# Linear attention and a routed expert layer in one kernel: the empty rows behind the whole second batch, the ramp's loads by two chunks, the first tokens' load between the two weights' loads, one chain of scales per expert

## The chip, the cores and the metric

The kernel runs on one core of one Trainium2 chip. The metric is the device time of one execution in microseconds; the median of three runs before is 392.27 us (391.34 to 393.69). Times below are in microseconds from the start of the profiled span unless they are durations.

## The reference

For 4 batches, 8 heads, 768 positions and a head size of 48, a gated linear attention runs over the positions, and its output, 3072 tokens of 384 values, goes through a layer of 8 experts, each token through one:

```python
f = 1.0 / (1.0 + np.exp(-f_logit))
for t in range(S):
    state = f[:, :, t, :, None] * state + np.einsum('bhd,bhe->bhde', k[:, :, t], v[:, :, t])
    y[:, :, t] = np.einsum('bhd,bhde->bhe', q[:, :, t], state)
# x = y with the heads side by side: 3072 x 384
e_idx = np.argmax(x @ w_gate, axis=1)          # the token's expert
gate_w = softmax(x @ w_gate)[e_idx]            # its scale, with
eom = sigmoid(x @ w_output_gate)[e_idx]        # the output gate's
h = np.maximum(x[mask] @ w1[e], 0.0)           # 384 -> 1024
out[mask] = gate_w * eom * (h @ w2[e])         # 1024 -> 384
```

## The kernel before

**The attention.** Each batch is cut into 6 chunks of 128 positions, so there are 24 chunks, numbered 0 to 23; chunks 0 to 5 are batch 0. Within a chunk a running product p of the forget gates and its counterpart i are made by scans, k is multiplied by i and q by p, and then the chunk is plain matmuls: scores (`qk`, L245), a causal mask, outputs from the state before and from the scores (`out_y`, L305 and L309), the chunk's contribution to the state (`state`, L278, with k transposed at L262), and a matmul that puts the heads side by side and makes the gates' logits at once (`x_tr`, L322). `prep(t)` holds a chunk's preparations as named steps: `s` (L197, ScalarE's sigmoid of the first position), `f` (L204, ScalarE's sigmoid of the others), `scan_p` and `scan_i` (VectorE), `mul_k` (L220) and `mul_q` (L223), on GpSimd from chunk 3 on.

The loop over t (L462) staggers this: iteration t computes the scores of chunk t, the outputs of chunk t-1 and the copies (`evac_y`, L316), state update (`state_upd`, L290 to L293) and turn of chunk t-2, and prepares t+1 to t+3. All engines keep the order in which the program is written: `chain` (L1047) binds each engine's instructions to it. So an instruction that waits holds back everything behind it on its engine.

**The loads.** All of them are issued on SyncE's queue in the order of the program. `load(b, cuts)` (L169) loads chunks c0 to c1 of the tensors named by letters: f, k, q by heads and positions, v by positions. Batch 0 and 1 are loaded ahead of the loop (L423 to L432), batches 2 and 3 in the loop, from iteration 3 on. Between the parts of batch 1 stand eight stores, one for each expert, that fill slots 256 to 511 of its place in a DRAM buffer `xs_dram` with rows marked empty (`clear`, L646). A DMA on this queue takes one of eight semaphores in turn, so that at most eight are under way.

**The routing.** When a group of chunks is through, each of its tokens has an expert and a slot among the expert's tokens (`route`, `slots`). From iteration 7 on a GpSimd scatter per chunk (`scatter`, L339) writes the chunk's 128 rows into `xs_dram`; it waits for the empty rows. The expert with the most tokens after 16 chunks is taken first; its weights w1 and w2 are loaded (`load(0, ...)`, L399, L609 and L621), four DMAs of 384 KB each, and when the scatters of the first 16 chunks are out, its first 256 tokens (`tokens_in`, L652). Its other tokens are loaded when all scatters have landed.

**The experts.** Weights and tokens are split into a high and a low part (`split`: a ScalarE cast, L631, and a subtraction, L632, on VectorE or GpSimd; `x_split`: L710 and L711), and each product is three matmuls. `mm1` (L754) makes one of 8 hidden blocks, with a ScalarE relu (L758) and a VectorE subtraction (L759) behind it and two PSUM buffers to do it in; `mm2` (L776) takes a hidden block to the outputs. The first expert is done in two parts: its early 256 tokens beside the end of the attention (`x_early`, `mm1_early`), then `AHEAD` blocks of their `mm2`, with the transposes of the late tokens (`x_late`) two blocks before their end, and then the late ones. While an expert's `mm2` runs, a list `front` of steps of the next one (splits of w1, transposes and splits of the tokens by `x_in`, L704) is worked off, one step per block. A token's scale is a chain of 13 small operations over all tokens of an expert (`gain_ops`, L680), mostly VectorE's, worked off a few at a time by `gain`; the first expert has two such chains, one for the early and one for the late tokens.

Of the kernel before, what the change touches and what calls it, by code (L numbers as in the profile page):

```python
# [21 lines left out]
C = 128  # L22
# [4 lines left out]
TS = 128  # L27
NT = 4
SLOTS = NT * TS
# [1 line left out]
EARLY = 256  # L31
T_TOP = 16
T_END = 20
AHEAD = 6
KC = DM // 128
KF = F // 128
BIG = 8192
# [4 lines left out]
RW = LG + 2 * E  # L42
# [3 lines left out]
HELD = 256  # L46
# [81 lines left out]
def attention(ctx, tc, nc, k, kpool, rt, q01, k01, f01, q23, k23, f23, v, wg, xs_dram, r, ex):  # L128
# [204 lines left out]
    def scatter(n):  # L333

        for _ in range(min(n, len(sq))):
            if sq[0] >= T_TOP and not ex.xg:
                return
            t = sq.pop(0)
            i = nc.gpsimd.indirect_dma_start(  # L339
                out=xs_dram, out_offset=bass.IndirectOffsetOnAxis(ap=r.slot[:, t:t + 1], axis=0),  # L340
                in_=xn[t // 4][:, t % 4, :], in_offset=None, bounds_check=E * N - 1, oob_is_err=False)
            for other in ex.apart:
                tc.declare_no_dep(i.ins, other.ins, reason="other slots")
            ex.apart.append(i)

# [42 lines left out]
    def top(ps):  # L388

        key = rt.tile([128, E], F32, name="key")  # L390
        mx = rt.tile([128, 1], F32, name="mx")
        nc.vector.scalar_tensor_tensor(out=key, in0=ps, scalar=float(E), in1=k.first_key, op0=ALU.mult, op1=ALU.add)
        dq[:0] = [
            lambda: nc.vector.tensor_reduce(out=mx, in_=key, axis=AX.X, op=ALU.max),
            lambda: nc.vector.tensor_tensor(out=r.top, in0=key, in1=mx.broadcast_to([128, E]), op=ALU.is_equal),
            lambda: nc.vector.tensor_tensor(out=key, in0=r.top, in1=k.num, op=ALU.mult),
            lambda: nc.vector.tensor_reduce(out=mx, in_=key, axis=AX.X, op=ALU.add),
            lambda: nc.vector.tensor_copy(out=r.top_id, in_=mx),
            lambda: ex.load(0, r.top_id[0:1, 0:1]),  # L399
        ]  # L400

    def slots(gi, t0, n):
# [17 lines left out]
    order = [(b, c) for b in range(B) for c in range(NCH)]  # L420
    last = len(order) - 1
    pre_of = [prep(t) for t in range(len(order))]
    load(0, [("fk", 0, 1), ("f", 1, 2), ("q", 0, 1), ("kq", 1, 2), ("f", 2, 4), ("v", 0, 2)])  # L423
    nc.sync.dma_start(out=turn[:, 0::2, 2 * D:XW], in_=wg[:, 0::2, 0:2 * E])
    for i in range(2):
        nc.sync.dma_start(out=turn[64 * i:64 * i + 64, 1::2, 2 * D:XW],
                          in_=wg[64 - 64 * i:128 - 64 * i, 1::2, 0:2 * E])
    load(0, [("kqv", 2, 4), ("fkqv", 4, 6)])
    load(1, [("fkqv", 0, 2), ("fkqv", 2, 4)])
    for e in range(E):  # L430
        ex.clear(e)
    load(1, [("fkqv", 4, 6)])  # L432

    def pre(t, *names):
        if hot(t):
# [26 lines left out]
    for t in range(last + 1):  # L462
# [3 lines left out]
        fill(more)  # L466
        if hot(t - 2):
            evac_y(t - 2, (1,))
        if t > 0:
            pre(t + 2, "f")  # L470
        if hot(t - 2):
            evac_y(t - 2, (0,))
            state_upd(t - 2)
        pre(t + 1, "mul_k")
        if t + 1 == last:
            done_sb.close()
# [34 lines left out]
            state(t - 1)  # L511
        run_pq(ready)
        if t == last:

            evac_y(t - 1)
            state_upd(t - 1)
            ex.x_early()
            for heads in ((0, 1, 4, 5), (2, 3, 6, 7)):
                out_y(t, heads)
            ex.split(1, 0, 2, nc.gpsimd)  # L520
# [3 lines left out]
        b, c = divmod(t - 3, NCH)  # L524
# [8 lines left out]
        if t >= T_END:  # L533
            scatter(2)
            if len(ex.apart) == T_TOP:
                ex.tokens_in(0, 0, EARLY // TS)
        if t + 1 == last:
            drain()
            assert ex.xg
            ex.split(1, 0, 0, nc.gpsimd)  # L540
# [32 lines left out]
class Experts:  # L573
# [4 lines left out]
    def __init__(self, tc, nc, k, r, raw, right, w1, w2, xs_dram, out, kp):  # L578
        self.tc, self.nc, self.k, self.r, self.raw, self.right, self.kp = tc, nc, k, r, raw, right, kp
        self.w1, self.w2, self.xs, self.out = w1, w2, xs_dram.rearrange("(e n) w -> e n w", e=E), out  # L580
        k.gain = kp.tile([TS, NT, E], F32, name="gain")
        k.dst = kp.tile([TS, NT, E], I32, name="dst")

        self.first = kp.tile([TS, NT, RW], F32, name="first_x")
        self.apart, self.number = [], {}
        self.wr, self.whl, self.todo, self.gq = {}, {}, [], []
        self.xg, self.xt, self.hs, self.ys, self.ysb = {}, {}, {}, {}, {}

# [50 lines left out]
    def clear(self, e):  # L639

        if e == 0:
# [1 line left out]
            self.nc.gpsimd.memset(self.empty, 0.0)  # L643
            self.nc.gpsimd.memset(self.empty[:, DM:DM + 1], float(BIG))
        n = (SLOTS - HELD) // TS
        self.nc.sync.dma_start(out=self.xs[e, HELD:SLOTS].rearrange("(j p) w -> p j w", p=TS),  # L646
                               in_=self.empty.unsqueeze(1).broadcast_to([TS, n, RW]))

    def tokens_in(self, s, j0, j1):
        early = s == 0 and j0 == 0  # L650
# [8 lines left out]
            self.apart.append(i)  # L659
        for j in range(j0, j1):  # L660
            self.xg[s, j] = (t[:, j - j0, :], min(TS, CAPS[s] - j * TS))
        self.meta = getattr(self, "meta", []) + [(s, j0, j1, t)]

    def gains(self):

# [192 lines left out]
    def run(self):  # L858
# [7 lines left out]
        for s in range(E):  # L866
# [7 lines left out]
            for f in range(KF):  # L874
                self.mm1(s, f)
                if s == 0:
                    self.gain(3)
                    if f > 2 and f % 2:
                        self.split(1, 1, f // 2 - 1, self.nc.gpsimd)
                if f % 2 == 0 and (2, s, f // 2) in self.wr:  # L880
                    self.split(2, s, f // 2, self.nc.gpsimd if s == 0 else None)
                if 1 <= f <= len(back):
# [1 line left out]
            front = [lambda i=i: self.split(1, s + 1, i) for i in range(KF // 2)  # L884
                     if (1, s + 1, i) in self.wr]
            for c in range(KC):
                front.insert(2 * c + 2 if s > 0 else len(front), lambda c=c: self.x_in(s + 1, c))
            if s + 1 == E:
                front = []
            self.gain(len(self.gq))  # L890
# [237 lines left out]
```

## Time and profile before

| | before |
|---|---|
| median of three runs | 392.27 us |
| the profiled execution, its span | 394.05 us, 392.3 us |
| granted TensorE clock, mean | 0.982 |
| TensorE busy | 365.1 us (93%) |
| VectorE, ScalarE, GpSimd busy | 235.6, 197.1, 150.7 us |
| moved by DMAs | 67.75 MB |

The profile is of one execution and has a time of its own, so parts of the span are set against 394.05 and not against the median. The attention takes the first 125 us or so, the first expert's early part runs from there to 148, its late part to 176, and the seven other experts the rest. Of the page's slices, the DMA row is at 0.9 from the second to the tenth of 40, and the granted clock at 0.9 or more but for the last.

### The profile page before, as it was taken

The numbers are of one execution on the slowest core, as the hardware profiler recorded it, in microseconds if no ns is written. First come the engines' busy times: TensorE is split into PE (matmuls) and PEld (weight loads), VectorE is DVE, ScalarE is ACT, GpSimd is POOL, SyncE is SP. The second block draws the span as 40 slices with busy tenths as digits, with TensorE's granted clock in tenths as the row PEclk, the third lists the DMA queues.
The fourth block names the chain that finished last, engine by engine and source line by source line (L and its number), as shares of the span: only waits on it lengthen the run. The fifth ranks groups of instructions, "written<-read, shape, count | busy, mean of one in ns | idle before, by whom it ended". The sixth has DMA issues, their size and how long they took to land.

```text
span 392.3 us, 8488 instructions
## 1 busy us (share of the span) xinstructions
PE 365.1 (93%) x3199; PEld 336.6 (86%) x3199; DVE 235.6 (60%) x495; ACT 197.1 (50%) x471; POOL 150.7 (38%) x180
## 2 busy tenths in 40 slices
PE   7799889999996999799999999999999999999990
PEld 3588778898886888799989999999999999999990
DVE  7878669898992764725644645454564565565500
ACT  3576466766754643415534634634644644654310
POOL 7676678899987650501201210310210310321011
PEclk9999989999999999989999999999999999999996
DMA  8999999999167139632535453544454454520010
GB/s 232 349 360 355 285 258 217 294 251 289 70 205 265 45 126 313 215 124 72 161 119 162 144 167 125 178 133 160 144 161 144 141 160 145 161 79 34 2 43 19
DMA packets 53427, 67.75 MB, mean 173 GB/s; under 512 B 3954, under 2 KB 48005, under 8 KB 53376
## 3 DMA queue, kind: packets, MB, share of 16 engines
q1 hardware_dynamic: 50064, 57.46, 50.0%
q0 software_dynamic: 3312, 9.65, 6.9%
q8 instruction: 27, 0.44, 0.5%
q14 instruction: 24, 0.20, 0.2%
HBM read 54.16 MB, written 13.39 MB: 172 GB/s over the span
## 4 chain that ended last, share of the span: by engine, by line
PE 65%; DMA 11%; DVE 6%; issue 6%; SPq 5%; POOL 3%; ACT 2%; POOLq 0%; DVEq 0%; ACTq 0%
PE h_ps L754 25%; PE y_ps L776 21%; PE y_ps L790 4%; SPq L182 4%; DMA f_t<-in_f 3%; PE x_ps L704 3%; PE x_ps L322 2%; DMA xs_dram<-empty 2%; PE o_ps L811 2%; DMA out<-o,dst 2%; DMA v_t<-in_v 2%; PE a_ps L245 2%; POOL xs_dram L339 2%; PE two_ps L309 1%; DVE p L209 1%
## 5 line engine op out<-in xcount | busy, mean ns | idle before, releaser
L819 POOL DMA_INDIRECT out<-o,dst x30 | 29.6, 987 | 188.7 <-ACT o L814 99.8
L759 DVE SCALAR_TENSOR_TENSOR hl<-h_ps,hh 128x256 fp32r<-128x256 f32 (+6 forms) x72 | 39.3, 546 | 51.7 <-ACT hh L758 51.3
L754 PE MATMUL h_ps<-xh,w1h 128*128 128x400 f32 (+6 forms) x192 | 67.4, 351 | 0.1
L754 PE MATMUL h_ps<-xh,w1l 128*128 128x400 f32 (+6 forms) x192 | 65.0, 338 | 0.0
L754 PE MATMUL h_ps<-xl,w1h 128*128 128x400 f32 (+6 forms) x192 | 64.9, 338 | 0.0
L758 ACT ACTIVATE hh<-h_ps 128x256 fp32r<-128x256 f32 (+6 forms) x72 | 34.7, 483 | 49.5 <-PE h_ps L754 47.9
L776 PE MATMUL y_ps<-hh,w2h 128*128 128x256 f32 (+4 forms) x168 | 58.2, 346 | 0.0
L776 PE MATMUL y_ps<-hl,w2h 128*128 128x256 f32 (+4 forms) x168 | 56.1, 334 | 0.0
L776 PE MATMUL y_ps<-hh,w2l 128*128 128x256 f32 (+4 forms) x168 | 56.1, 334 | 0.0
L711 DVE TENSOR_TENSOR xl<-x_ps,xh 128x400 fp32r<-128x400 f32 (+6 forms) x23 | 13.1, 568 | 42.8 <-ACT xh L710 39.5
L754 PEld LDWEIGHTS h_ps<-xh,w1h 128*128 128x128 f32 x192 | 36.1, 188 | 1.0 <-DVE hl L759 0.3
L754 PEld LDWEIGHTS h_ps<-xl,w1h 128*128 128x128 f32 x192 | 36.2, 188 | 0.4
L754 PEld LDWEIGHTS h_ps<-xh,w1l 128*128 128x128 f32 x192 | 36.0, 188 | 0.5
L710 ACT CAST xh<-x_ps 128x400 fp32r<-128x400 f32 (+6 forms) x23 | 11.2, 489 | 48.8 <-PE x_ps L704 42.3
L223 POOL TENSOR_TENSOR q_t<-q_t,p 128x512 f32<-128x512 f32 x24 | 31.6, 1315 | 8.0 <-DMA q_t<-in_q 5.1
L776 PEld LDWEIGHTS y_ps<-hh,w2h 128*128 128x128 f32 x168 | 32.0, 191 | 1.1
L632 DVE TENSOR_TENSOR w2l<-w2r,w2h 128x768 fp32r<-128x768 f32 x31 | 30.1, 971 | 4.2 <-ACT w2h L631 1.6
L776 PEld LDWEIGHTS y_ps<-hl,w2h 128*128 128x128 f32 x168 | 32.1, 191 | 0.5
L776 PEld LDWEIGHTS y_ps<-hh,w2l 128*128 128x128 f32 x168 | 32.1, 191 | 0.4
L245 PE MATMUL a_ps<-q_t,k_t 64*128 64x128 f32 x384 | 28.0, 285 | 4.5 <-POOL q_t L223 2.9
L322 PE MATMUL x_ps<-turn,xt 128*128 128x112 f32 x192 | 26.6, 283 | 5.1 <-ACT xt L316 5.1
L209 DVE TENSOR_TENSOR_SCAN p<-f_ps,start_p 128x511 f32<-128x511 f32 x22 | 28.0, 1273 | 3.0 <-ACT f_ps L204 1.6
(176 smaller groups left out, 781.7 us busy)
## 6 DMA issues: line engine op xcount, KB each, us to landing
w1r<-in_w SPq DMA_DIRECT2D x32, 384.0 KB, 3.8
w2r<-in_w SPq DMA_DIRECT2D x32, 384.0 KB, 3.1
v_t<-in_v SPq DMA_DIRECT2D x12, 512.0 KB, 9.2
xg<-xs_dram SPq DMA_DIRECT2D x5, 802.0 KB, 6.5
xs_dram<-empty SPq DMA_DIRECT2D x8, 401.0 KB, 11.1
f_t<-in_f SPq DMA_DIRECT2D x5, 512.0 KB, 9.8
k_t<-in_k SPq DMA_DIRECT2D x5, 512.0 KB
q_t<-in_q SPq DMA_DIRECT2D x5, 512.0 KB, 10.0
```

The costliest lines, as they stand in the source:

```text
L182: nc.sync.dma_start(out=t[:, :, sl], in_=first[b, :, :, sl].rearrange("g p s -> p g s"))
L209: nc.vector.tensor_tensor_scan(out=flat(d["p"])[:, 1:n], data0=flat(d["f"])[:, 0:n - 1], data1=sp[:, 1:n], initial=sp[:, 0:1], op0=ALU.mul ...
L223: nc.gpsimd.tensor_tensor(out=q_t[i][:, :, sl], in0=q_t[i][:, :, sl], in1=d["p"], op=ALU.mult)
L245: nc.tensor.matmul(aps[t][par][:, g, :], k_t[b % 2][r, g, sl], q_t[b % 2][r, g, sl], start=(g == 0), stop=(g == NP - 1))
L322: nc.tensor.matmul(xps[t][:, g, :], xt[t][:, g, :], turn[:, g, :], start=(g == 0), stop=(g == NP - 1))
L632: (eng or self.nc.vector).tensor_tensor(out=flat(lo), in0=flat(t), in1=flat(hi.bitcast(F32)), op=ALU.subtract)
L754: nc.tensor.matmul(ps[:, 0:n], a[:, c, cs], b, start=(i == 0), stop=(i == 3 * KC - 1))
L758: nc.scalar.activation(out=hi, in_=ps[:, 0:n], func=AF.Relu)
L759: nc.vector.scalar_tensor_tensor(out=lo, in0=ps[:, 0:n], scalar=0.0, in1=hi.bitcast(F32), op0=ALU.max, op1=ALU.subtract)
L776: self.nc.tensor.matmul(self.ys[d][:, c0:c0 + n], a[:, f % 2, ds], b, start=(f == 0 and i == 0 and part == 0), stop=(f == KF - 1 and i == ...
L790: nc.tensor.matmul(ps[0:n, 0:DM], a, b[:, f % 2, :], start=(i == 0), stop=(i == 3 * KF - 1))
L819: self.nc.gpsimd.indirect_dma_start(out=self.out, out_offset=bass.IndirectOffsetOnAxis(ap=self.k.dst[0:n, j, s:s + 1], axis=0), in_=t[0:n] ...
```

## The change

1. The ramp: batch 0 is loaded by two chunks from the start, f ahead of q and k, and q and k of chunks 2 and 3 move ahead of the gates' weights.
2. The empty rows are stored after the last load of batch 1. The scatters of chunks 0 and 1 are declared independent of them, since a token of the first 256 can't have a slot behind 255.
3. In iteration 2 the sigmoid of chunk 4 moves behind both copies and the state update of chunk 0.
4. The first expert's w2 is loaded after its first tokens, which now stand between w1 and w2.
5. In the last iteration a scatter of two chunks is put ahead of the copies.
6. The first expert has one chain of scales over all its tokens; two of its steps are taken per block, not three. Two of the second expert's w1 splits are done in this part, on VectorE, where three were done on GpSimd; the other two go to the front list, with the tokens' steps between and behind them.
7. AHEAD is 8 and not 6: all of the early tokens' `mm2` stands ahead of the late ones' `mm1`.

```diff
-AHEAD = 6
+AHEAD = 8
...
@@ scatter
-            for other in ex.apart:
+
+            for other in ex.apart + (ex.cleared if (t + 1) * C <= HELD else []):
                 tc.declare_no_dep(i.ins, other.ins, reason="other slots")
...
@@ top
-            lambda: ex.load(0, r.top_id[0:1, 0:1]),
+            lambda: ex.load(0, r.top_id[0:1, 0:1], rest=False),
...
@@ the loads ahead of the loop
-    load(0, [("fk", 0, 1), ("f", 1, 2), ("q", 0, 1), ("kq", 1, 2), ("f", 2, 4), ("v", 0, 2)])
+    load(0, [("fqk", 0, 2), ("f", 2, 4), ("v", 0, 2), ("qk", 2, 4)])
     nc.sync.dma_start(out=turn[:, 0::2, 2 * D:XW], in_=wg[:, 0::2, 0:2 * E])
...
-    load(0, [("kqv", 2, 4), ("fkqv", 4, 6)])
-    load(1, [("fkqv", 0, 2), ("fkqv", 2, 4)])
+    load(0, [("v", 2, 4), ("fkqv", 4, 6)])
+    load(1, [("fkqv", 0, 2), ("fkqv", 2, 4), ("fkqv", 4, 6)])
     for e in range(E):
         ex.clear(e)
-    load(1, [("fkqv", 4, 6)])
...
@@ the loop
-        if t > 0:
+        if t not in (0, 2):
             pre(t + 2, "f")
         if hot(t - 2):
             evac_y(t - 2, (0,))
             state_upd(t - 2)
+        if t == 2:
+            pre(4, "f")
...
         if t == last:
+            scatter(2)
 
             evac_y(t - 1)
...
                 ex.tokens_in(0, 0, EARLY // TS)
+                ex.load_rest(0)
...
@@ tokens_in
-        self.meta = getattr(self, "meta", []) + [(s, j0, j1, t)]
+        if not early:
+            self.meta = getattr(self, "meta", []) + [(s, 0, j1, t if s > 0 else self.first)]
...
@@ run, the hidden blocks of the first expert
                 if s == 0:
-                    self.gain(3)
-                    if f > 2 and f % 2:
-                        self.split(1, 1, f // 2 - 1, self.nc.gpsimd)
+                    self.gain(2)
+                    if f in (3, 5):
+                        self.split(1, 1, f // 2 - 1)
...
-                front.insert(2 * c + 2 if s > 0 else len(front), lambda c=c: self.x_in(s + 1, c))
+                front.insert(2 * c + 2 if s > 0 else 2 * c + 1, lambda c=c: self.x_in(s + 1, c))
```

More of the change, by code (lines that the diff above doesn't have):

```diff
@@ L584, in __init__ @@
         self.first = kp.tile([TS, NT, RW], F32, name="first_x")
-        self.apart, self.number = [], {}
+        self.apart, self.cleared, self.number = [], [], {}
         self.wr, self.whl, self.todo, self.gq = {}, {}, [], []
@@ L645, in clear @@
         n = (SLOTS - HELD) // TS
-        self.nc.sync.dma_start(out=self.xs[e, HELD:SLOTS].rearrange("(j p) w -> p j w", p=TS),
-                               in_=self.empty.unsqueeze(1).broadcast_to([TS, n, RW]))
+        i = self.nc.sync.dma_start(out=self.xs[e, HELD:SLOTS].rearrange("(j p) w -> p j w", p=TS),
+                                   in_=self.empty.unsqueeze(1).broadcast_to([TS, n, RW]))
+        self.cleared.append(i)
     def tokens_in(self, s, j0, j1):
```

## The prediction

> **What bounds the kernel now.** I read the page's busy shares, then the timeline of TensorE for its idle gaps, then the timelines of the engine that ended each gap, the DMA issues, and a table by stretches of time. TensorE is busy 365.1 us of 392.3, so all there is to win outside of less work is the 27 us of idle time. These are its gaps that the change can touch (start, duration, engine, line, tiles, and in brackets the idle time before and who ended it):
>
> ```profile
> 17.29 1.16 PE L245 MATMUL a_ps<-q_t,k_t 64*128 64x128 f32 x16 [1.99 <-POOL q_t L223]
> ...
> 20.36 1.15 PE L322 MATMUL x_ps<-turn,xt 128*128 128x112 f32 x8 [1.32 <-ACT xt L316]
> ...
> 50.40 2.04 PE L322 MATMUL x_ps<-turn,xt 128*128 128x112 f32 x8 [2.97 <-ACT xt L316]
> ...
> 61.31 1.04 PE L322 MATMUL x_ps<-turn,xt 128*128 128x112 f32 x8
> ...
> 75.79 0.44 PE L309 MATMUL two_ps<-at,v_t 128*64 128x128 f32 x4
> ...
> 126.80 0.63 PE L704 MATMUL x_ps<-ident,first_x 128*128 128x128 f32 x4 [1.90 <-DMA first_x<-xs_dram]
> ...
> 147.99 0.44 PE L704 MATMUL x_ps<-ident,first_x 128*128 128x128 f32 x2 [1.81 <-DMA first_x<-xs_dram]
> ...
> 166.08 0.85 PE L704 MATMUL x_ps<-ident,xg 128*128 128x128 f32 x4 [1.89 <-DVE xl L711]
> ```
>
> The six gaps sum to 11.9 us. Two cost more than their length. Behind 2.97 us idle the eight x_ps matmuls took 2.04 us, where undisturbed ones take 1.04. The table by stretches (length; busy time of PE, PEld, DVE, ACT, POOL; granted clock, DMA share, GB/s) has the clock:
>
> ```profile
> 5.00:10.00 5.00, 4.05 (x22) 1.84 (x22) 4.83 (x7) 1.23 (x6) 3.14 (x17) 1.00 1.12 324
> 20.00:25.00 5.00, 4.64 (x76) 4.19 (x77) 4.11 (x7) 3.66 (x13) 3.96 (x5) 1.00 1.08 358
> 48.00:58.00 10.00, 7.60 (x96) 6.79 (x100) 5.88 (x9) 6.18 (x20) 7.66 (x8) 0.83 1.09 273
> 160.00:170.00 10.00, 8.11 (x52) 6.95 (x50) 6.08 (x16) 3.69 (x10) 3.90 (x3) 0.83 0.68 206
> ```
>
> A mean of 0.83 over 10 us is 1.7 us of clock lost, behind the gap at 50 and again behind the one at 166, and nowhere near the gaps of 1.8 to 2.0 us at 17, 127 and 148. So the gap at 50 costs 4.7 us and the one at 166 costs 3.6. The DMA share of 1.08 and 1.09 says that the 16 engines are full from the start into the third batch.
>
> **The change part by part.** A and B are the loads, C and D the tokens on their way into the first expert, E the turn to the second expert.
>
> A, the ramp. Chunk 2 waits for q behind single-chunk loads; then chunk 0's output copy waits behind a sigmoid that in its turn waits.
>
> ```profile
> 15.54 1.69 POOL L223 TENSOR_TENSOR q_t<-q_t,p 128x512 f32<-128x512 f32 x1 [2.76 <-DMA q_t<-in_q]
> ```
> ```profile
> 19.41 0.60 ACT L204 ACTIVATE f_ps<-f_t 128x508 f32<-128x508 f32 x1 [0.32 <-DVE i L216]
> 19.94 0.36 ACT L316 COPY xt<-two_ps 128x256 f32<-128x256 f32 x1
> ...
> 48.79 0.21 ACT L197 ACTIVATE start_p<-f_t 128x4 f32<-128x4 f32 x1 [3.96 <-DMA f_t<-in_f]
> ...
> 58.23 0.22 ACT L197 ACTIVATE start_p<-f_t 128x4 f32<-128x4 f32 x1
> ```
>
> With q of chunks 2 and 3 ahead of the gate weights the first wait goes; swapping the sigmoid behind the copies takes the second. Against it, the first sigmoid waits for 512 KB instead of 256, some 0.7 us at 358 GB/s. I take 1.8 of the 3.3 us (bounds: -0.7 and 3.3).
>
> B, the empty rows. Their eight stores of 401 KB each stand in SyncE's queue ahead of the first batch-1 load of chunks 4 and 5, which ScalarE waits for at 48.79:
>
> ```profile
> 27.77 8.30 SPq L646 DMA_DIRECT2D xs_dram<-empty x8
> 37.20 0.38 SPq L182 DMA_DIRECT2D f_t<-in_f  x1
> ...
> 45.50 1.79 SPq L185 DMA_DIRECT2D f_t<-in_f  x2
> ...
> 65.78 2.56 SPq L178 DMA_DIRECT2D v_t<-in_v  x3
> ...
> 112.87 2.79 SPq L621 DMA_DIRECT2D w2r<-in_w  x4
> 119.33 24.29 SPq L652 DMA_DIRECT2D first_x<-xs_dram  x2
> ```
>
> Moved behind these four loads, the stores take away the whole wait, 4.7 us. But no byte is saved, and the queue is full: the next loads, of batch 2, still come behind both. So I ask what is late next. The issues at 45.50 and at 65.78 (first of each row) landed after
>
> ```profile
> DMA to landing us min/median/max: 10.3/10.3/10.3
> ```
> ```profile
> DMA to landing us min/median/max: 7.9/7.9/7.9
> ```
>
> that is at 55.8 (its second half, issued about a microsecond later, near 56.8) and at 73.7. Their users: ScalarE takes chunk 12's f at 58.23, TensorE its v at 75.79. At 48.79 ScalarE's start came 1.6 us before TensorE's restart at 50.40; f at 56.8 would let the x_ps matmuls of 61.31 start at 58.4, so f caps the gain at 2.9 us, and v caps it at 75.79 - 73.7 = 2.1, as long as the loads land when they did. A and B ask for 6.5 together; they get 2.1 plus what the loads themselves gain. That is +0.5 (1.57 MB of first loads in rows of double length, at 358 instead of 324 GB/s) and +1.8 (2.1 MB of batch-1 loads at 358, ahead of the stores, instead of 273 behind them), and less 1.0 for the first two scatters, which no longer wait for the stores and so go in among them: the page gives 54 scatters 6.9% of the span, 0.5 us each.
>
> ```profile
> q0 software_dynamic: 3312, 9.65, 6.9%
> ```
>
> ```profile
> 60.12 1.29 POOL L220 TENSOR_TENSOR k_t<-k_t,i 128x512 f32<-128x512 f32 x1
> ```
>
> The third scatter does wait for the stores, which I now put near 54 (the batch-2 landing at 55.8 less the 1.3), so GpSimd stands there with the product for chunk 11's k behind it. That ran at 60.12 before, 56.7 with the gain below, so it is covered unless the stores are 3 us late. A and B: 2.1 + 1.3 = 3.4 us (bounds: 1.6, if the slow stretch belongs to the data and stays, and 6.5, if the loads keep up). [...]
>
> C, the first tokens' load. It is issued at 119.33, when the scatter it waits for has landed, behind 1.5 MB of w2 issued from 112.87, and lands at 126.7, 7.3 us on. The second load of the same size finds the queue empty:
>
> ```profile
> 143.25 4.70 DMA first_x<-xs_dram
> ...
> 170.06 6.62 PE y_ps L776 x54
> ```
>
> With w2 behind it I take 4.7, and the scatter lands sooner too: 124.0 or earlier, and TensorE is free at 126.80 - 1.90 = 124.9. Next in its way is the state that the last chunk's output reads:
>
> ```profile
> 125.69 0.36 DVE L293 TENSOR_TENSOR state<-misc,pend 128x192 f32<-128x192 f32 x1
> ```
>
> Six transposes at 0.63 for four end at 125.8, the state at 126.05, so C gives 1.5 and not 1.9 (bounds 0 and 1.9). w2, moved past this load, is issued near 119; its first use is ScalarE's cast at 129.64, and four issues of 0.7 us (2.79 / 4) and a landing within 5 end by 127, so it is covered.
>
> ```profile
> 129.64 0.84 ACT L631 CAST w2h<-w2r 128x768 fp32r<-128x768 f32 x1
> ```
>
> ```profile
> 129.83 1.82 POOL L632 TENSOR_TENSOR w1l<-w1r,w1h 128x768 fp32r<-128x768 f32 x1 [3.92 <-ACT w1h L631]
> ```
>
> The scatters of chunks 18 and 19 (two of some 1.3 us) move up into these 3.92 us of GpSimd and cost nothing; the later ones wait for a cast that follows TensorE, so the last tokens come 1.5 earlier with it.
>
> D, AHEAD. One hidden block's nine matmuls cost 6.62 x 9 / 54 = 1.1 us; two blocks put ahead of the late tokens' transposes cover 2.2 of the 1.81 us gap: gain 1.8 (0.7, if the tokens do not move up with C). The work itself is only moved.
>
> E, the second expert's tokens. What held TensorE at 166.08 is VectorE, late behind two chains of scales and a GpSimd split:
>
> ```profile
> 162.27 1.83 DVE L693 TENSOR_SCALAR g_sm<-g_sm 128x2 f32<-128x2 f32 x1
> ...
> 164.44 0.96 DVE L632 TENSOR_TENSOR w1l<-w1r,w1h 128x768 fp32r<-128x768 f32 x1
> ```
> ```profile
> 162.24 1.83 POOL L632 TENSOR_TENSOR w1l<-w1r,w1h 128x768 fp32r<-128x768 f32 x1 [0.24 <-ACT w1h L631]
> ```
>
> An operation on two elements took 1.83 us, exactly as long as GpSimd's split beside it. Afterwards there is one chain of 13 steps for two, no GpSimd split in this stage, and the three token blocks stand one or more blocks apart. The gap and its clock, 3.6, go. In return two splits of 0.96 move onto VectorE between the hidden blocks; the first pushes one block's subtraction back by some 0.7 us, which TensorE feels; the second finds room. E gives 2.9 (bounds: 1.4, if both splits are felt whole and the last block waits 0.25; 3.6). [...] The rows at 50 and 166 throttled after 2.97 and 1.89. [...]
>
> The sum is 3.4 + 1.5 + 1.8 + 2.9 = 9.6 us. The profiled execution took 394.05 us for its span of 392.3; less 9.6 that is 384.5. It lies 1.8 above the median of the runs shown, 392.27, so the median becomes 382.7.
>
> **The rivals.** *The loads keep up.* Then A and B give 6.5, the sum 12.7, the time 379.6. For it: the stretch at 48 to 58 runs at 273 GB/s, far below 358, perhaps only because loads and stores mix. Against: slack of 2.1 us before any change.
>
> *The starvation only moves.* TensorE then stands before chunk 12 as it did before chunk 10, with half a clock behind it again (1.7); A and B give nothing, the rest 6.2: 386.1. For it: the DMA share of 1.09. [...]
>
> *VectorE becomes the bound of the first expert's late half.* Both splits are felt, the tokens' gap stays, E gives 0 and D 0.7: 392.27 - 5.6 = 386.7. For it: VectorE is what held TensorE here before; against it: its scales are halved and GpSimd no longer stops it.
>
> *Slower: the stores now starve batch 2.* They stand directly ahead of it. To cancel 6.2 us and the 2.1 of slack, batch 2 must land 8.3 us later than before, so the 3.2 MB of stores would have to take 22 us (9 at 358 GB/s, 8.3, and what the loads gain), below 150 GB/s. The worst full stretch shown has 273. At 130 GB/s they take 24.6, and the time is 394.9.
>
> *It does not do what it says:* the waits named are not the last ones, a second wait is right behind each, and the time is 391 to 393.
>
> **How the numbers follow.** Forecast 0.52, loads keep up 0.18, starvation moves 0.14, VectorE bound 0.07, slower 0.04, no effect 0.05. The likeliest is 382.7, by its own bounds 380 to 385.5; 378.5 to 388 holds the first four cases, all but about 0.1. Half a per cent (2 us) is about what a measurement of this kernel can tell from no change: faster 0.90, same 0.06, slower 0.04.
>
> **What would show it.** A: no gap over 1 us near 17 and 20. B: no wait of ScalarE for f of chunk 10, and a wait for a batch-2 load near 53 to 73 in its place; none there means the first rival. C: first_x lands within 5 us of its issue and its transposes wait for nothing. D: no wait for first_x at the late tokens. E: no gap over 0.5 us at xg, clock 1.00 around it, w1l on VectorE at 0.96. A gap over 3 us with a clock below 0.9 anywhere from 50 to 80, or a new gap before the hidden blocks, would make the prediction wrong.

## The result and the profile after

The changed kernel takes 382.25 us (median of 4 runs, 381.79 to 382.55), the kernel before, timed beside it, 392.98 us (391.34 to 395.27). The ratio is 0.9722, with a 95% interval of 0.9668 to 0.9775. Executions more than 1.5% above the fastest of their kernel in one comparison are left out of all medians and ranges here; only the kernel before had any, 4 of its 42. The forecast was 382.7 us with a range of 378.5 to 388.0. The profiled execution took 382.55 us for a span of 380.8 us; the one before took 394.05 for 392.3. So there are 11.5 us to account for in the two profiles, against the 9.6 of the forecast.

I read the two traces by milestones: the start of a matmul that each kernel has once. These are rows of TensorE's timeline of the kernel before: scores of chunks 8, 9 and 23, the outputs of the last chunk, the first hidden block of the late tokens, and the second expert's first one.

```profile
45.68 1.16 PE L245 MATMUL a_ps<-q_t,k_t 64*128 64x128 f32 x16
...
55.09 1.16 PE L245 MATMUL a_ps<-q_t,k_t 64*128 64x128 f32 x16
...
120.11 1.16 PE L245 MATMUL a_ps<-q_t,k_t 64*128 64x128 f32 x16 [0.80 <-POOL k_t L220]
...
127.57 0.65 PE L305 MATMUL f_ps<-q_t,state 64*64 64x128 f32 x8
...
150.86 0.28 PE L754 MATMUL h_ps<-xh,w1h 128*128 128x256 f32 x1
...
176.52 0.37 PE L754 MATMUL h_ps<-xh,w1h 128*128 128x448 f32 x1
```

The same six of the changed kernel, and with them the gaps that answer to those of the forecast (16.69, 19.48, 119.85, 141.75 and 161.09) and the turn of chunk 8 (56.28), which comes in the iteration that prepares chunk 12:

```profile
16.69 1.60 PE L245 MATMUL a_ps<-q_t,k_t 64*128 64x128 f32 x16 [0.23 <-ACT kn L270]
...
19.48 1.15 PE L322 MATMUL x_ps<-turn,xt 128*128 128x112 f32 x8 [0.61 <-ACT xt L316]
...
45.36 1.16 PE L245 MATMUL a_ps<-q_t,k_t 64*128 64x128 f32 x16
...
49.99 1.16 PE L245 MATMUL a_ps<-q_t,k_t 64*128 64x128 f32 x16
...
56.28 1.15 PE L322 MATMUL x_ps<-turn,xt 128*128 128x112 f32 x8
...
115.20 1.16 PE L245 MATMUL a_ps<-q_t,k_t 64*128 64x128 f32 x16 [0.81 <-POOL k_t L220]
...
119.85 0.63 PE L710 MATMUL x_ps<-ident,first_x 128*128 128x128 f32 x4
...
121.19 0.65 PE L305 MATMUL f_ps<-q_t,state 64*64 64x128 f32 x8 [0.49 <-DVE state L293]
...
141.75 0.38 PE L710 MATMUL x_ps<-ident,first_x 128*128 128x128 f32 x2
...
144.56 0.28 PE L760 MATMUL h_ps<-xh,w1h 128*128 128x256 f32 x1
...
161.09 0.75 PE L710 MATMUL x_ps<-ident,xg 128*128 128x128 f32 x4 [0.23 <-DVE xl L717]
...
165.05 0.36 PE L760 MATMUL h_ps<-xh,w1h 128*128 128x448 f32 x1
```

| up to | before | after | ahead by | its part |
|---|---|---|---|---|
| scores of chunk 8 | 45.68 | 45.36 | 0.3 | A 0.3 |
| scores of chunk 9 | 55.09 | 49.99 | 5.1 | |
| scores of chunk 23 | 120.11 | 115.20 | 4.9 | B 4.6 |
| outputs of chunk 23 | 127.57 | 121.19 | 6.4 | C 1.5 |
| late tokens' first block | 150.86 | 144.56 | 6.3, and 2.2 of work done earlier | D 2.1 |
| second expert's first block | 176.52 | 165.05 | 11.5 | E 3.0 |
| end of the span | 392.3 | 380.8 | 11.5 | |

The 2.2 us are the two `mm2` blocks that AHEAD moves ahead of the late tokens; the chain of waits has them as one piece:

```profile
142.57 2.16 PE y_ps L782 x18
```

The table by stretches shows TensorE without a gap from 48 to 58 and the clock at 1.00 where it was 0.83 (length; busy time of PE, PEld, DVE, ACT, POOL; granted clock, DMA share, GB/s):

```profile
40.00:45.00 5.00, 5.00 (x84) 4.51 (x76) 4.79 (x12) 3.89 (x13) 4.12 (x5) 1.00 1.09 341
45.00:50.00 5.00, 5.00 (x91) 4.47 (x87) 4.42 (x8) 3.44 (x10) 3.79 (x5) 1.00 1.07 237
48.00:58.00 10.00, 10.00 (x170) 8.77 (x170) 8.37 (x15) 6.68 (x22) 9.59 (x10) 1.00 1.11 257
55.00:70.00 15.00, 14.82 (x233) 12.97 (x231) 13.22 (x27) 10.96 (x34) 13.16 (x15) 1.00 1.10 280
160.00:170.00 10.00, 9.78 (x66) 8.99 (x65) 5.53 (x15) 4.37 (x9) 0.00 (x0) 1.00 0.36 121
```

and the stretches of the kernel before that answer to three of them:

```profile
40.00:45.00 5.00, 5.00 (x80) 4.43 (x78) 4.80 (x12) 3.91 (x13) 4.09 (x5) 1.00 1.10 234
45.00:50.00 5.00, 2.43 (x43) 2.00 (x39) 1.66 (x4) 1.13 (x5) 2.13 (x3) 1.00 1.08 349
55.00:70.00 15.00, 14.82 (x251) 13.31 (x247) 13.58 (x29) 10.34 (x32) 12.27 (x14) 1.00 1.10 238
```

The slow five microseconds of some 235 GB/s are there in both, before at 40 to 45 and after at 45 to 50: they go with the last of the stores, wherever these stand. What differs is the stretch behind, 280 GB/s for 238.

The engines that ended the old gaps, in their timelines after (ScalarE, VectorE, SyncE's queue, GpSimd):

```profile
5.10 0.60 ACT L204 ACTIVATE f_ps<-f_t 128x508 f32<-128x508 f32 x1 [2.80 <-DMA f_t<-in_f]
...
5.86 1.28 DVE L209 TENSOR_TENSOR_SCAN p<-f_ps,start_p 128x511 f32<-128x511 f32 x1 [2.38 <-ACT start_p L197]
...
41.77 1.90 SPq L185 DMA_DIRECT2D f_t<-in_f  x2
...
54.67 0.21 ACT L197 ACTIVATE start_p<-f_t 128x4 f32<-128x4 f32 x1 [1.42 <-DMA f_t<-in_f]
...
141.41 0.27 POOL L687 TENSOR_SCALAR dst<-first_x 128x4 int32<-128x4 f32 x1 [4.03 <-DMA first_x<-xs_dram]
```

ScalarE does wait for a load of batch 2 now: the 1.42 us in front of 54.67, for f of chunk 12. But its copy for the turn of chunk 8 still comes in time: TensorE starts that at 56.28 with no idle time in front. The late tokens are there at 141.4, 0.3 us ahead of TensorE.

### The profile page after: what moved, and what is told of

It reads as the page before. It is cut to its first block, busy times and chain, and to the rows that moved or that the text cites. A ratio compares the mean times of both kernels' runs of the same rounds, so it can differ in the third digit from the quotient of the medians.

```text
span 380.8 us, 8463 instructions
## 1 busy us (share of the span) xinstructions
PE 361.7 (95%) x3199; PEld 334.2 (88%) x3199; DVE 234.8 (62%) x488; ACT 196.8 (52%) x468; POOL 146.7 (39%) x176
## 4 chain that ended last, share of the span: by engine, by line
PE 78%; DVE 9%; ACT 3%; issue 3%; DMA 3%; POOL 2%; POOLq 0%; DVEq 0%; ACTq 0%
PE h_ps L760 28%; PE y_ps L782 22%; PE x_ps L322 5%; PE y_ps L796 4%; PE a_ps L245 3%; PE x_ps L710 3%; PE two_ps L309 2%; DVE p L209 2%; DVE i L216 2%; PE o_ps L817 2%; PE two_ps L305 2%; PE one_ps L309 2%; PE kn_ps L262 2%; PE one_ps L278 2%; DMA out<-o,dst 2%
## 5 line engine op out<-in xcount | busy, mean ns | idle before, releaser
L825 POOL DMA_INDIRECT out<-o,dst x30 | 31.7, 1058 | 187.8 <-ACT o L820 118.6
L223 POOL TENSOR_TENSOR q_t<-q_t,p 128x512 f32<-128x512 f32 x24 | 30.6, 1276 | 6.1 <-DVE p L209 5.9
L245 PEld LDWEIGHTS a_ps<-q_t,k_t 64*128 64x128 f32 x384 | 23.7, 187 | 7.1 <-POOL q_t L223 2.0
```

The costliest lines, as they stand in the source:

```text
L223: nc.gpsimd.tensor_tensor(out=q_t[i][:, :, sl], in0=q_t[i][:, :, sl], in1=d["p"], op=ALU.mult)
L245: nc.tensor.matmul(aps[t][par][:, g, :], k_t[b % 2][r, g, sl], q_t[b % 2][r, g, sl], start=(g == 0), stop=(g == NP - 1))
L825: self.nc.gpsimd.indirect_dma_start(out=self.out, out_offset=bass.IndirectOffsetOnAxis(ap=self.k.dst[0:n, j, s:s + 1], axis=0), in_=t[0:n] ...
```

## The experiments

The runs undo one part each, or do one part alone. "After" is 382.25 us, and a run's price is its median less that. It was not timed again beside them, and its own four runs span 0.8 us, so a price under half a microsecond can't be told from nothing. The kernel before, timed beside each group of runs, had medians of 392.97 to 393.2. Two parts of the change were not undone by any run: the moved sigmoid (3) and the earlier scatter in the last iteration (5).

**The stores back between the parts of batch 1**, with the exemption of the first scatters kept:

```diff
-    load(1, [("fkqv", 0, 2), ("fkqv", 2, 4), ("fkqv", 4, 6)])
+    load(1, [("fkqv", 0, 2), ("fkqv", 2, 4)])
     for e in range(E):
         ex.clear(e)
+    load(1, [("fkqv", 4, 6)])
```

> The changed kernel with the eight stores of empty rows put back ahead of the last four loads of batch 1. Theory 'the loads keep up': the changed trace has TensorE at chunk 9's scores at 49.99 against 55.09 before, and at 45.36 against 45.68 one chunk earlier, so the stores alone were worth 4.8; put back they cost 4.8: 387.0, with a gap of about 3 us near 50 and the half clock behind it if the idle window falls so (3.0 without it: 385.3). Rival, the forecast's cap: A and B together were held to some 3.4 by batch 2, so putting one of them back costs 3.4 or less: 385.7 or below.

Measured: 385.27 us (384.44 to 386.47), 3.0 more. ScalarE waits again for f of chunk 10, and TensorE behind it:

```profile
47.68 0.21 ACT L197 ACTIVATE start_p<-f_t 128x4 f32<-128x4 f32 x1 [3.48 <-DMA f_t<-in_f]
...
49.29 1.74 PE L322 MATMUL x_ps<-turn,xt 128*128 128x112 f32 x8 [2.49 <-ACT xt L316]
```

By its time alone the run does not decide, since 385.27 fits both the theory without the half clock (385.3) and the rival (385.7 or below). The trace does: from the scores of chunk 8 to those of chunk 9 it takes 8.94 us (45.05 to 53.99) and 4.63 in the changed kernel, so the stores' place is worth 4.3 there, more than the rival's 3.4. With the wait that comes back, B's mechanism is shown. The runs differ by 2 us among themselves; in the profiled one, the longest, the clock behind the gap is lower (0.97 from 45 to 50, 0.69 from 50 to 55: 1.7 us of clock lost).

**The stores moved alone**, in the kernel before (with the exemption; all else as it was):

```diff
...
-    load(1, [("fkqv", 0, 2), ("fkqv", 2, 4)])
+    load(1, [("fkqv", 0, 2), ("fkqv", 2, 4), ("fkqv", 4, 6)])
     for e in range(E):
         ex.clear(e)
-    load(1, [("fkqv", 4, 6)])
```

> The kernel before with one part of the change alone: the stores behind the whole second batch, and the first two scatters independent of them. Theory 'the loads keep up': 4.8 less than before, 387.5 to 388.2, no gap of TensorE between 45 and 110 above 0.8. Rival, the cap of the forecast: the first loads of batch 2 land too late for chunk 12 without the ramp's longer rows, a gap of 1 to 3 us near 56 to 62, and 2 to 3.4 less than before.

Measured: 391.4 us (387.28 to 393.05 over 10 runs), ratio 0.9931 [0.9893, 0.997], only 1.7 us less than before, and less of a gain than both the theory and the rival had. The profiled run (393.05 us) shows why this isn't the price of B:

```profile
21.33 1.16 PE L322 MATMUL x_ps<-turn,xt 128*128 128x112 f32 x8 [1.85 <-ACT xt L316]
...
48.20 1.16 PE L245 MATMUL a_ps<-q_t,k_t 64*128 64x128 f32 x16
52.84 1.16 PE L245 MATMUL a_ps<-q_t,k_t 64*128 64x128 f32 x16
```
```profile
20.00:25.00 5.00, 3.67 (x38) 3.21 (x40) 3.77 (x6) 2.90 (x9) 4.08 (x6) 0.73 1.08 357
```

From chunk 8 to 9 it takes 4.64 us where before took 9.41: B's 4.8 us are there in full, with no cap from batch 2 and with the old rows of the ramp. Chunk 8 itself starts at 48.20 in place of 45.68: by the turn of chunk 0 the ramp is 1.0 us late (21.33 for 20.36), and its gap of 1.85 us has half a clock behind it (0.73 from 20 to 25). The gap of 1.96 us in front of the late tokens (145.15) has one too (0.83 from 140 to 150). Gaps of that length had half a clock behind them in some places and not in others (last section). The ten runs differ with their granted clocks: the three with the highest granted clock (0.989 to 0.991) took 387.28 to 388.14 us, about what the theory had, and the five with the lowest (0.978) took 391.24 to 393.05.

**Four more stores** behind the eight (1.64 MB to rows that no token uses):

```diff
+        if e < 4:
+            self.cleared.append(self.nc.sync.dma_start(
+                out=self.xs[e, 2 * SLOTS:2 * SLOTS + SLOTS - HELD].rearrange("(j p) w -> p j w", p=TS),
+                in_=self.empty.unsqueeze(1).broadcast_to([TS, n, RW])))
```

> The changed kernel with four more stores of empty rows, to places that nothing reads, behind the first ones (1.6 MB more; the result is the same). In the changed trace ScalarE waits 1.4 us for chunk 12's f at 54.67 and TensorE has no gap, so the slack there is about nil. Theory 'just in time': batch 2 lands later by the stores' 1.64 MB at 230 to 350 GB/s, 4.7 to 7.1 us, and all of it is seen as a gap of TensorE near 57, with the half clock behind it (1.7): 386.9 to 391. Rival 'the loads have room': at most 2 us: 382.2 to 384.2.

Measured: 390.05 us (389.49 to 391.43), 7.8 more. Now the starvation is there, at chunk 12 as the forecast's rival had it, and with a gap of 5.72 us:

```profile
61.93 2.05 PE L322 MATMUL x_ps<-turn,xt 128*128 128x112 f32 x8 [5.72 <-ACT xt L316]
```

ScalarE gets f of chunk 12 at 60.32 in place of 54.67, 5.65 us later, and the turn of chunk 8 starts 5.65 us later (61.93 for 56.28). So batch 2 comes just in time in the changed kernel: the whole delay shows at TensorE. It is less than the 6.9 us that 1.64 MB take at the 237 GB/s of that stretch; the rest of the 7.8 goes with the half clock behind the gap (0.52 from 60 to 65, 0.80 from 65 to 70).

**The first two scatters wait for the empty rows again:**

```diff
-            for other in ex.apart + (ex.cleared if (t + 1) * C <= HELD else []):
+            for other in ex.apart:
```

> The changed kernel without the exemption of the first two scatters: they wait for the empty rows again, as all later ones do. With the stores behind the whole batch they land near 52.5, and the first scatter stands at 46.3 in GpSimd's order with the products for k and q of chunk 9 behind it. Theory (a wait takes the place of the one removed; the exemption belongs to B): GpSimd stands some 6 us, the scores of chunk 9 start near 53.8 in place of 50.0, and the time is 385 to 388, the upper end if the clock is halved behind the gap. Rival (GpSimd has that much room, or the stores land sooner): the scores of chunk 9 start by 51, and 382.2 to 383.

Measured: 389.33 us (388.8 to 390.7), 7.1 more, above what was expected. GpSimd stands until 52.5 with chunk 9's products behind it. The row puts the wait down to VectorE's `p`, but the edit brings back the wait for the stores, and in the changed kernel the last of them lands at 52.07, by SyncE's queue:

```profile
52.51 1.23 POOL L339 DMA_INDIRECT xs_dram<-xn,slot  x1 [7.41 <-DVE p L209]
...
55.09 2.08 PE L245 MATMUL a_ps<-q_t,k_t 64*128 64x128 f32 x16 [5.08 <-POOL k_t L220]
```

5.1 us are the gap, and by the scores of chunk 10 the run is 6.9 late (61.56 against 54.62), with the half clock behind the gap (0.72 from 50 to 55, 0.80 from 55 to 65). Without the exemption B would have lost more than the 4.6 us it gained: the two edits are one.

**The ramp's old loads** in the changed kernel:

```diff
-    load(0, [("fqk", 0, 2), ("f", 2, 4), ("v", 0, 2), ("qk", 2, 4)])
+    load(0, [("fk", 0, 1), ("f", 1, 2), ("q", 0, 1), ("kq", 1, 2), ("f", 2, 4), ("v", 0, 2)])
...
-    load(0, [("v", 2, 4), ("fkqv", 4, 6)])
+    load(0, [("kqv", 2, 4), ("fkqv", 4, 6)])
```

> The changed kernel (382.25 us) with the first batch's loads cut as they were before: the first two chunks one by one, and q and k of chunks 2 and 3 behind the gates' weights. The sigmoid of chunk 4 stays behind the copies. The step at stake is A, of which the trace of the changed kernel shows 0.3 us by chunk 8. Theory (VectorE's scans set the ramp, which start 1 us earlier with single-chunk loads, and what is saved at the q of chunk 2 is lost there): the scan chain starts near 4.8, the gap in front of the scores of chunk 2 comes back at about 2 us, the scores of chunk 8 start at 45.4 to 45.9, and the time is 382.3 to 382.8. Rival (the longer rows of the ramp are what brought batch 2's loads forward, as the prediction's +0.5 has it): f of chunk 12 lands half a microsecond or more after 54.6, TensorE gets a gap in front of the turn of chunk 10 near 56, and the time is 383 to 384. Rival 2 (the forecast's 1.8): 384.0.

Measured: 383.11 us (382.8 to 384.68), 0.9 more. Chunk 8 starts at 46.21, 0.85 later, and the span is 0.6 longer. f of chunk 12 lands when it did:

```profile
54.60 0.21 ACT L197 ACTIVATE start_p<-f_t 128x4 f32<-128x4 f32 x1 [0.51 <-DMA f_t<-in_f]
```

So the longer rows did not bring batch 2 forward, which refutes the forecast's +0.5, though the time falls among those of that rival. VectorE's scans start at 4.82, as early as before, but lose most of that in one instruction:

```profile
7.59 1.26 POOL L223 TENSOR_TENSOR q_t<-q_t,p 128x512 f32<-128x512 f32 x1 [1.62 <-ACT pend L226]
7.61 1.79 DVE L220 TENSOR_TENSOR k_t<-k_t,i 128x512 f32<-128x512 f32 x1
```

In the kernel before, with the same loads, the same two instructions came out the other way round:

```profile
7.62 0.69 DVE L220 TENSOR_TENSOR k_t<-k_t,i 128x512 f32<-128x512 f32 x1
7.62 1.82 POOL L223 TENSOR_TENSOR q_t<-q_t,p 128x512 f32<-128x512 f32 x1 [1.65 <-ACT pend L226]
```

With a second such loss (1.03 us at 12.10) VectorE comes to chunk 2 at 13.05, no earlier than in the changed kernel (13.01). The 0.85 us come behind that, with the late q of chunk 2: its product on GpSimd starts at 15.50 for 14.36, VectorE's product for k beside it takes 1.49 us for 0.69, and TensorE waits 1.03 us at 17.53.

**f alone by single chunks**, ahead of q and k, a try at a better ramp:

```diff
-    load(0, [("fqk", 0, 2), ("f", 2, 4), ("v", 0, 2), ("qk", 2, 4)])
+    load(0, [("f", 0, 1), ("f", 1, 2), ("qk", 0, 2), ("f", 2, 4), ("v", 0, 2), ("qk", 2, 4)])
```

> The changed kernel with f of chunks 0 and 1 loaded as two single chunks ahead of q and k, which stay in one load of two chunks each. Theory (A brought little because f for two chunks lands 1 us later, and VectorE's scans, which set the ramp, start that much later): f lands near 4.0, the scan chain starts near 4.8 and not at 5.9, every chunk of the ramp comes 0.6 to 1.0 us earlier, and the time is 381.3 to 381.7, ahead of both kernels. Rival (what is won in the ramp is lost at batch 2, whose loads land just in time at 54.6): a gap of up to 1 us in front of the turn of chunk 10 near 55, and 382.2. Rival 2 (the ramp is set by k and GpSimd or the gates' weights, not by VectorE): the scores of chunk 2 start where they did, 16.7, and 382.2.

Measured: 383.26 us (382.36 to 384.18), 1.0 more. The scans do start at 4.81, but k is next in the way: VectorE waits 2.08 us for it, and its product starts at 9.64, where the changed kernel has it at 8.65; TensorE is idle for 2.94 us in front of the first scores, which then take 1.80 us and 1.16 in the changed kernel. The first part of the theory held (f sets the start of the scans), the second didn't (that this is worth a microsecond). The order f, k, q by itself was not tried.

**w2 ahead of the first tokens** again:

```diff
-            lambda: ex.load(0, r.top_id[0:1, 0:1], rest=False),
+            lambda: ex.load(0, r.top_id[0:1, 0:1]),
...
-                ex.load_rest(0)
```

> The changed kernel with the first expert's w2 loaded right behind its w1, ahead of the first tokens. Theory: the first tokens then land 7.3 us after their issue again and TensorE waits 1.9 us for them; the late tokens follow and stay hidden: +1.5, 383.7. Rival: the late tokens, whose scatters sit behind casts that follow TensorE, are what counts, and they land when they did, so that the wait only moves and the time stays at 382.2.

Measured: 383.32 us (382.81 to 383.81), 1.1 more. The gap is back, with the clock at 1.00 around it:

```profile
121.51 0.63 PE L709 MATMUL x_ps<-ident,first_x 128*128 128x128 f32 x4 [1.90 <-DMA first_x<-xs_dram]
```

**AHEAD back to 6:**

```diff
-AHEAD = 8
+AHEAD = 6
```

> The changed kernel with AHEAD 6. In the changed trace the late tokens' first reader on GpSimd starts at 141.41 and TensorE's transposes at 141.75 without a wait; two blocks earlier TensorE would be there at 139.6. Theory: it waits 1.8 us, 384.0, and if the idle window falls so, half a clock more (up to 385.7). Rival: the late tokens come early enough since w2 is out of their way, no wait, 382.2.

Measured: 384.92 us (384.05 to 386.2), 2.7 more. Here the gap has half a clock behind it, which is what the price has above 1.8:

```profile
141.16 0.44 PE L710 MATMUL x_ps<-ident,first_x 128*128 128x128 f32 x2 [1.82 <-DMA first_x<-xs_dram]
```
```profile
141.10:144.50 3.40, 3.34 (x19) 3.35 (x20) 1.18 (x3) 1.02 (x3) 0.26 (x1) 0.61 0.95 311
```

**E's three parts, one by one.** The two w1 splits back on GpSimd; two chains of scales and three steps per block; the second expert's tokens behind its splits:

```diff
-                        self.split(1, 1, f // 2 - 1)
+                        self.split(1, 1, f // 2 - 1, self.nc.gpsimd)
```

> The changed kernel with the two w1 splits in the first expert's late part on GpSimd instead of VectorE, all else as changed. Theory: a GpSimd split of 1.83 us holds up small VectorE operations beside it, so VectorE is late at the first token block and TensorE waits some 0.5 to 1.5 us more at or before xg: 382.7 to 383.7. Rival: with one chain of scales VectorE has room for it and loses two splits of 0.96, so the time stays or falls by the 0.35 us that TensorE waits for a subtraction at 151.7: 381.9 to 382.2.

```diff
-        if not early:
-            self.meta = getattr(self, "meta", []) + [(s, 0, j1, t if s > 0 else self.first)]
+        self.meta = getattr(self, "meta", []) + [(s, j0, j1, t)]
...
-                    self.gain(2)
+                    self.gain(3)
```

> The changed kernel with two chains of scales for the first expert (early and late tokens apart, three steps per block), the splits and the front list as changed. Theory: 13 more steps of 0.2 us on VectorE between the hidden blocks push the subtractions back, 26 steps in 8 blocks; TensorE loses 1 to 2 us there: 383.2 to 384.2. Rival: VectorE has the room, and the second chain is not what held the tokens: 382.2.

```diff
-                front.insert(2 * c + 2 if s > 0 else 2 * c + 1, lambda c=c: self.x_in(s + 1, c))
+                front.insert(2 * c + 2 if s > 0 else len(front), lambda c=c: self.x_in(s + 1, c))
```

> The changed kernel with the second expert's three token blocks at the end of the front list again (split, split, then three token blocks one after another). Theory: a token block needs its cast and subtraction (0.53 + 0.62 and two hops, 1.4 us) before the next may take the one PSUM buffer, and a block of mm2 is 1.1 us, so two waits of some 0.3 us: 382.8, no clock loss. Rival: the order was the main part of E: the 1.9 us gap at xg comes back, with the half clock: 384 to 385.9.

Measured: 382.26 us (382.18 to 382.47), 382.64 (382.09 to 383.14) and 382.36 (382.27 to 382.42): 0.0, 0.4 and 0.1 more. From the late tokens' first block to the second expert's it is 20.6, 20.8 and 20.6 us, and 20.5 in the changed kernel. None of the three brings the gap back, and all three are faster than their theories had them.

**All of E undone** (the three edits above together, with GpSimd's third split):

```diff
-                    if f in (3, 5):
-                        self.split(1, 1, f // 2 - 1)
+                    if f > 2 and f % 2:
+                        self.split(1, 1, f // 2 - 1, self.nc.gpsimd)
```

> The changed kernel with the whole of E undone: two chains of scales in the first expert, three steps per block, three of the second expert's splits on GpSimd, and all of its tokens' steps behind the splits. Undone one by one these cost 0.4, 0.0 and 0.1 us. Theory (the gap in front of the second expert's tokens needs them together, VectorE's late chain and the GpSimd splits beside it): a gap of 1.5 to 2 us there, 20.5 us from the late tokens' first hidden block to the second expert's become 23 to 23.5, and the time is 384.3 to 385.5, higher if the clock is halved behind it. Rival (the parts add): 382.8 and no gap above 0.6. Rival 2 (the gap was itself due to where the early tokens' last blocks stood, so that D removed it): 382.3.

Measured: 384.19 us (384.1 to 385.34), 1.9 more, and 22.3 us for that stretch. The parts don't add (0.5); together they make the gap, and the scale's two-element operation is again as long as the split beside it:

```profile
155.54 1.83 POOL L636 TENSOR_TENSOR w1l<-w1r,w1h 128x768 fp32r<-128x768 f32 x1 [0.25 <-ACT w1h L635]
155.56 1.84 DVE L698 TENSOR_SCALAR g_sm<-g_sm 128x2 f32<-128x2 f32 x1
...
159.38 0.75 PE L709 MATMUL x_ps<-ident,xg 128*128 128x128 f32 x4 [1.89 <-DVE xl L716]
```
```profile
160.00:165.00 5.00, 4.97 (x38) 4.47 (x38) 2.69 (x10) 1.17 (x3) 0.00 (x0) 1.00 0.72 242
```

The gap is as long as before's, 1.89 us, but the clock stays at 1.00, so it costs 1.9 and not 3.

The prices of the parts undone one at a time are 0.9 (ramp's loads), 3.0 (stores), 1.1 (first tokens), 2.7 (AHEAD) and 1.9 (E): 9.6 us of the 10.7 between the medians, with the half clocks that some of the gaps drew. No version here beats the changed kernel.

## Why the prediction was right, and where its steps were not

**The whole.** The median is 0.4 us below the forecast, but the sum was 9.6 and the profiles have 11.5. The difference is A and B together, 4.9 for 3.4; D gave 0.3 and E 0.1 more. That the median still came out so near is luck: the profiled execution before lay 1.8 above the median that the forecast started from, the one after only 0.3 above its own, which takes back 1.5 of the 1.9. Such differences between runs of one kernel are most likely the clock's, an estimate from the ten runs of the stores moved alone (0.978 with 391.24 to 393.05 us, 0.989 to 0.991 with 387.28 to 388.14).

**A: 0.3 for 1.8, the step mis-sized.** Both old gaps shrank as the forecast said (1.99 to 0.23 us, 1.32 to 0.61). But its price for the first sigmoid's later f, "some 0.7 us", was 1.03 (5.10 for 4.07), and it was set off against TensorE's gaps, as if it could only eat part of them. It moved the start of VectorE's scans from 4.83 to 5.86. The scores of chunk 0 start no later for that (9.44 for 9.49, since GpSimd's product for q held them before), but those of chunk 1 do, by 1.2 us. The kernel before, and then the changed one with its wait:

```profile
12.03 1.16 PE L245 MATMUL a_ps<-q_t,k_t 64*128 64x128 f32 x16
```
```profile
13.23 1.16 PE L245 MATMUL a_ps<-q_t,k_t 64*128 64x128 f32 x16 [1.18 <-DVE k_t L220]
```

By the turn of chunk 0 the changed kernel is 0.9 us ahead (19.48 for 20.36). One turn later half of that is gone: there ScalarE's second copy stands behind the sigmoid of chunk 5, which now waits for VectorE's scan as the sigmoid of chunk 4 did before:

```profile
23.71 0.60 ACT L204 ACTIVATE f_ps<-f_t 128x508 f32<-128x508 f32 x1 [0.57 <-DVE i L216]
...
24.66 1.15 PE L322 MATMUL x_ps<-turn,xt 128*128 128x112 f32 x8 [0.29 <-ACT xt L316]
```

The forecast read the two gaps that the change could touch and not the chain behind them. The 0.3 itself is uncertain: nine runs above have the changed kernel's ramp, and their chunk 8 starts between 45.05 and 45.61. How much of A is the loads and how much the moved sigmoid stays partly open: undoing the loads costs 0.9 us, but part of that is the chance of the two instructions at 7.6, and no run has the sigmoid alone back.

**B: 4.6, near the 4.7 asked; the cap is the step that failed.** The forecast capped A and B at 2.1 + 1.3, since the loads of batch 2 would land when they had landed before, but for 1.3. They landed earlier. f of chunk 12 is there at 54.6 in place of the 56.8 that the forecast reckoned, 2.2 us sooner; with the forecast's own 2.9 for f that is 5.1, and the turn of chunk 8 moved by 61.31 - 56.28 = 5.0. f was the next limit, as argued, with the wrong time. v, from which the 2.1 came, did not limit at all: it was issued at 62.62 in place of 65.78, and its first use, at 70.87, waits for nothing. The step at fault is to take a landing time from the old trace for a load whose issue waits for something that the change moves. For f that is the landing of the stores, whose semaphores the loads of batch 2 take next. Of the waits of SyncE's queue in the changed kernel:

```profile
SPq L185 <- DMA xs_dram<-empty: 8.9, 8, 1.9
```

The two halves of f are issued at 41.77 and 43.34, as the first and the second store land (41.71 and 43.32). Before, with four loads between the stores and f, the first half had the semaphore of the fifth store, which landed at 44.25, and was issued at 45.50, behind an issue of v that took 3.20 us.

Of the terms of the 1.3, the +0.5 for longer rows is refuted (with the old ramp f of chunk 12 lands when it did). The +1.8 had its reason wrong: the slow stretch goes with the stores and has only moved. Why the batch-2 loads run at 280 GB/s and not 238 from 55 to 70 is open: moving the stores alone has it too (290), but so has the changed kernel with the stores put back (271), so their place can't be the whole reason. From 40 to 70 the share of the 16 DMA engines is as high in both kernels (1.07 to 1.11 in the stretches above): B's 4.6 us came with the engines as busy as before.

**The rivals.** *The loads keep up* is what came for B, without A's part: its 6.5 needed both. *The starvation only moves* is half right: ScalarE does wait for batch 2, and 1.64 MB more bring the gap at TensorE. Missing among the rivals was the scatter: without the exemption the change would have lost B and more, and the forecast priced the exemption at its side effect (1.0) alone. It placed the stores' landing at 54; 52.5 is where GpSimd was released in the run without the exemption, and the third scatter, at 55.17 in the changed kernel, finds them done.

**C: 1.5, as forecast, and for its reason.** The first tokens' time from issue to landing, among the operations of their tile:

```profile
DMA to landing us min/median/max: 5.1/5.1/5.1
```

That is a little over the 4.7 that the forecast took and the 5 of its sign, and early enough: the load was issued at 114.40, and TensorE takes the tokens at 119.85 without a wait. The next thing in TensorE's way is the state, 0.49 us at 121.19, as the forecast had it.

**D: 2.1 for 1.8.** TensorE doesn't wait for the late tokens; the margin is 0.3 us.

**E: 3.0 for 2.9.** The gap is 0.23 us and the clock 1.00. The forecast took for granted that its causes add; each alone costs at most 0.4 us, all of them 1.9, and the rest of the 3.0 goes with the half clock, which the kernel before had there (0.83 from 160 to 170) and the run with all of E undone did not (1.00 from 155 to 165).

## What to carry to other kernels

When a stall is removed, ask for each later load not only when it landed, but what its issue waited for: here the queue has at most eight DMAs under way, an issue waits for an earlier landing (41.77 for 41.71), and so the loads moved with the queue and their old landing times were no cap. A change that gives a whole queue a new order needs the waits on the moved transfers looked at too; here the two scatters decide the sign of B. Where several causes make one gap, undo them together as well as one by one.

## What the hardware showed that was not expected

**Gaps of one length had half a clock behind them in one place and not in another.** These are gaps of TensorE of 1.8 us and more, and what came behind them:

| idle, us | kernel, start of the matmuls behind it | granted clock | clock lost, us |
|---|---|---|---|
| 5.72 | four more stores, 61.93 | 0.52 from 60 to 65, 0.80 from 65 to 70 | 3.4 |
| 5.08 | scatters wait, 55.09 | 0.72 from 50 to 55, 0.80 from 55 to 65 | 3.4 |
| 2.97 | before, 50.40 | 0.83 from 48 to 58 | 1.7 |
| 2.49 | stores back, 49.29 | 0.97 from 45 to 50, 0.69 from 50 to 55 | 1.7 |
| 1.99 | before, 17.29 | 1.00 from 10 to 30 | none |
| 1.96 | stores moved alone, 145.15 | 0.83 from 140 to 150 | 1.7 |
| 1.90 | before, 126.80 | 1.00 from 55 to 166 | none |
| 1.90 | w2 ahead of the first tokens, 121.51 | 1.00 from 115 to 130 | none |
| 1.89 | before, 166.08 | 0.83 from 160 to 170 | 1.7 |
| 1.89 | all of E undone, 159.38 | 1.00 from 155 to 165 | none |
| 1.85 | stores moved alone, 21.33 | 0.73 from 20 to 25, 0.93 from 25 to 30 | 1.7 |
| 1.82 | AHEAD 6, 141.16 | 0.61 from 141.1 to 144.5, 0.89 from 144.5 to 148 | 1.7 |
| 1.81 | before, 147.99 | 1.00 from 55 to 166 | none |

Behind the gap of 2.94 us with f by single chunks (10.43) the scores took 1.80 us for 1.16. So a gap of 1.8 to 2.0 us cost either its length or some 1.7 us more, and the four of 2.49 us or more in the table all had clock lost behind them.

In the kernel before the clock is 0.50 for 3.41 us from 50.44 and again from 166.49; the two starts are 116.05 us apart, 34.0 times 3.41. Cut into stretches of that length on this grid (what two of the expectations call the idle window), its trace has these as the ones in which TensorE is idle longest, up to 375 us:

| stretch, before | TensorE idle, us | granted clock in the next stretch |
|---|---|---|
| 47.03 to 50.44 | 2.97 | 0.50 |
| 163.08 to 166.49 | 1.89 | 0.50 |
| 146.01 to 149.42 | 1.81 | 1.00 |
| 16.31 to 19.72 | 1.66 | 1.00 |
| 125.53 to 128.94 | 1.26 | 1.00 |

The gap of 1.89 us lies whole in one of these stretches, while the grid cuts the one of 1.99 us into 1.01 and 0.98 and the one of 1.90 us into 0.64 and 1.26. So in this trace the half clock came behind the two stretches with the most idle time, and where a gap lay counted beside its length. Why that is so is not shown. Both kernels end at half clock, where TensorE runs out of work (0.50 from 384.95 us before and from 373.50 after); up to 365 us the changed kernel has 1.00 throughout. In the page's row of the clock by slices, the two stretches at half clock of the kernel before are the two 8s, so its last slice is not the only one under 0.9. With the granted clocks of the stores moved alone this is the likely reason, by estimate, that kernels with such gaps vary from run to run (before 388.46 to 393.89 over 9 runs in one comparison) and the changed one, with none longer than 1.5, hardly does (381.79 to 382.55).

**Two instructions that start within 20 ns of each other came out in two ways, a microsecond apart on VectorE.** The products for k on VectorE and q on GpSimd at 7.6 us took 0.69 and 1.82 us in the kernel before, and 1.79 and 1.26 with the ramp's old loads. VectorE's starts first in neither (7.62 beside 7.62, 7.61 beside 7.59), and what decides it is not shown. An operation of VectorE on two elements took as long as GpSimd's split beside it, 1.83 and 1.83 us before, 1.84 and 1.83 with all of E undone.
